# Row maxima in an adaLN block's projection phase: whole chains, more pairs, and the next task for a new K tile

## The chip, the core and the metric

The kernel runs on one core of one Trainium2 chip. The metric is the device time of one execution in microseconds (us). A core has the engines TensorE (PE, with its weight loads PEld), VectorE (DVE), ScalarE (ACT), GpSimd (POOL) and SyncE (SP, which issues most DMAs).

## The reference, cut to what matters

```python
mod = (_silu(c) @ w_mod).reshape(c.shape[0], 6, 1, -1)      # sa, ca, ga, sb, cb, gb
h = _layernorm(x) * (1 + ca) + sa
q, k, v = (h @ wqkv) in 16 heads of 28                       # x: 2048 tokens x 448
p = softmax(q k^T * 28 ** -0.5)                              # over all 2048 keys
x = x + ga * ((p v) @ wo)
h = _layernorm(x) * (1 + cb) + sb
x = x + gb * (gelu(_layernorm(h) @ w1 + b1) @ w2 + b2)       # 448 -> 1792 -> 448
```

All is in fp32. The kernel splits each fp32 operand into a rounded part, hi (fp32r), and the rest, lo, and adds up hi x hi, hi x lo and lo x hi.

## The kernel before, in words

**Phases.** Phase one makes Q, K and V; the attention follows, and the MLP at its end. The 2048 tokens are four blocks of 512 (b = 0 to 3), the 16 heads four groups of four (g = 0 to 3). A group's four heads lie at partitions 0, 32, 64 and 96 (j = 0 to 3).

**Tasks of phase one** (loop at L901). A task of block b makes one tile of Q (kind 0) or K (kind 1) of one group (`qk_task`), or 128 tokens of V (kind 2, `v_task`), by a chain of 11 matmuls on PE (L464, `mm_acc`). Block 0 has 13 tasks, blocks 1 and 2 have 11 each, block 3 has 8; the number within the block is n. The last two tasks of a block but the last make Q and K of group 0 for the next block. In blocks 1 and 2 tasks 5 to 8 are those on V, and tasks 4 to 7 also prepare a piece of the next block's normalised input (`h_chunk`: ACT scales and casts it, POOL makes its lo part). In block 0 the first three chains are computed ahead of the loop. For blocks 2 and 3 the input comes transposed; DVE takes the statistics (`ln1_cols`, L214 and L215) two blocks ahead, one step per task, the last step (`rows_out`) sends mean and scale through DRAM into rows, and POOL applies them (L333, L334) at tasks 1, 2, 4 and 5 (`APPLY_AT`) of the block before.

**Row maxima.** The softmax needs each row's maximum over the keys. It is taken ahead of the attention, from the hi parts: a single maximum (`max_one`) is one matmul of 28 rows (L544, 128 queries against 512 keys of one head) and one DVE reduction (L549). A unit is one group with one block of queries, written (g, qt), in all 16; with 4 blocks of keys, 4 rows of queries and 4 heads there are 1024 maxima. A pair of maxima (`pair_diff`) takes two key blocks A and B at once: a matmul against B - A (`k_diff`, made by POOL), a Relu on ACT (L557), a matmul against A, and one DVE instruction that adds both and reduces (L561): max(A, B) = A + relu(B - A). So a pair costs two matmuls, as two singles do, one ACT and one DVE instruction. `paired` names the units whose first two key blocks go so in phase one; they wait in `pxq`, the others in `mxq`.

**How many, and where.** Behind each chain `emit_task(n, sixth, n_pairs)` puts n maxima's worth of work (P1RATE = 4 in block 0, 5 later; one more, in the PSUM tile `o`, where `sixth` is set and there is a pair): the matmuls of the pairs' differences, then singles, then the pairs' second matmuls. Five PSUM tiles serve them in turn (`mx_ring`: ma, ma, m2, m2, m1). `p1_n` carries its settings. In tasks 1, 3 and 5 of block 1 `emit_mid` puts four more maxima into the middle of the chain. `queue_max` offers a new K tile's maxima; the loop calls it after the next task's `emit_task`, so the offer serves the task after that.

**Attention.** 256 steps, 16 for each unit, at each a tile of scores (L1453, 12 matmuls), two exponentials (L1466), and the product with V of the step before (L1408). What maxima phase one left are done inside the steps. Up to step RING - 1 a step has four single matmuls, or three and a pair's difference. From step RING = 121 (the ring form) it has one single and one double, two matmuls into a two-bank tile with one DVE reduction of 1024 columns (L757). In the last steps there are none left and three score tiles take turns. `load_hi` brings the hi tiles of the next group from DRAM and lets their maxima be used 3 steps later, or 5 in the ring form.

Of the kernel before, what the change touches and what calls it, by code (L numbers as in the profile page):

```python
# [14 lines left out]
F32R = mybir.dt.float32r  # L15
# [19 lines left out]
APPLY_AT = (1, 2, 4, 5)  # L35
RING = 121
MOD_AT = 124
# [10 lines left out]
def tile_adaln_block(ctx: ExitStack, tc: tile.TileContext, x, x_t, wqkv, wo, w1, b1, w2, b2, c, w_mod, out):  # L48
# [410 lines left out]

    def mm_acc(p, terms, mid=None):  # L460
        for i, (a, b) in enumerate(terms):
            if mid and i == len(terms) // 2:
                mid()
            pe.matmul(p, a, b, start=(i == 0), stop=(i == len(terms) - 1))  # L464
# [18 lines left out]
    def qk_task(b, kind, g, begun=None):  # L483
        p, ts = begun or qk_terms(b, kind, g)
        if begun is None:
            mm_acc(p, ts, p1_n[3])
        emit_task(*p1_n[:3])
        if g == 0:
            tg = ("kh" if kind else "qh") + str(b)
            hi = sb.tile([128, 512], F32R, tag=tg, name=nm(tg), bufs=1)  # L490
            (kh_sb if kind else qh_sb)[(g, b)] = hi
        elif g == 1 and b < 2:

            hi = sbt("raw" if kind else "osb", [128, 512], F32R, bufs=3 if kind else 2)
            (kh_sb if kind else qh_sb)[(g, b)] = hi
        else:
            hi = sbt("hi", [128, 512], F32R, bufs=3)
        full = sbt("full", [128, 512], bufs=3)
        lo = sbt("lo", [128, 512], F32R, bufs=3)
        act.copy(full, p)  # L500

        def split():
            (act.copy if b else dve.tensor_copy)(hi, full)
            if kind == 1 and (g, b) == (0, 1):
                k_diff.append(sbt("raw", [128, 512], F32R, bufs=3))
                pool.tensor_tensor(out=k_diff[0], in0=f(hi), in1=f(kh_sb[(0, 0)]), op=ALU.subtract)
            pool.tensor_tensor(out=lo, in0=full, in1=f(hi), op=ALU.subtract)
            sl = slice(b * 512, (b + 1) * 512)
            for part, t in enumerate((hi, lo)):
                sp.dma_start(f(dscr[kind][part][g])[:, sl], f(t))  # L510

            if b < 3 or g == 0 or (kind, g) == (0, 1):
                put_spare()
            spare.append((kind, g, sl))

        return split

    def v_task(b, t, p):
# [3 lines left out]
            lambda k: hh(k)[:, ts], lambda k: hl(k)[:, ts], lambda k: wv[0][:, k, :], lambda k: wv[1][:, k, :],  # L522
        ), p1_n[3] if phase1[0] else None)
        if phase1[0]:
# [7 lines left out]
    pxq = []  # L532
    k_diff = []
    paired = ((0, 1), (0, 2), (0, 3))
    px_no = [0]
# [17 lines left out]
    def pair_diff(g, qt, i, j):  # L553
        m = max_mm(g, qt, i, j, k_diff[0])
        r = d0(1 + px_no[0] % 3)
# [208 lines left out]
    def emit_task(n, sixth, n_pairs):  # L764
# [8 lines left out]
        for x in range(n_ops - len(pairs)):  # L773
            if mxq:
                near = [m for m in mxq[:24] if not p1_n[4] or m[:2] == mxq[0][:2]]
                want = free[x % len(free)] if free else x % 4
# [21 lines left out]
    p1_n = [0, False, 1, None, False]  # L798

# [94 lines left out]
    for b in range(NB):  # L894
# [11 lines left out]
        for n, (tb, kind, g) in enumerate(tasks):  # L906
# [8 lines left out]

            k = n - (6, 4, 4, 4)[b]
# [694 lines left out]
```

## Time and profile before

| | |
|---|---|
| time, median of 3 runs | 1087.91 us (1087.47 to 1088.52) |
| the profiled execution's time | 1088.08 us |
| its span | 1086.3 us |
| busy: PE, DVE, ACT, POOL | 1077.9, 801.0, 691.2, 251.2 us |
| phase one ends (first score matmul) | 158.67 us |
| granted TensorE clock | 1.0 |

A row of a timeline gives the start, the length, the engine, the line, what is written and read, the shapes and the number merged; in brackets stands the idle time ahead of it and what ended it. Matmuls overlap, so PE's lengths do not add up; starts are what counts. A row of windows gives the stretch, its length, then busy time and count of PE, PEld, DVE, ACT and POOL, then clock, DMA share and GB/s.

### The profile page before, as it was taken

How to read it: one execution, taken by the hardware profiler on the slowest of the kernel's cores; microseconds unless marked ns; L12 is line 12 of the kernel's file. 1: busy time of each engine (PE TensorE's matmuls, PEld its weight loads, DVE VectorE, ACT ScalarE, POOL GpSimd, SP SyncE). 2: the span in 40 equal slices, each digit the busy share in tenths (PEclk: the TensorE clock that was granted, in tenths of full speed). 3: DMA queues.
4: the chain of work that ended last, by engine and by line, in shares of the span. 5: the costliest groups of instructions: out<-in, count | busy, mean ns of one | idle time of the engine just before them, and what ended most of it. 6: DMA issues, size and time to landing. Idle time of an engine off the chain costs nothing.

```text
span 1086.3 us, 20646 instructions
## 1 busy us (share of the span) xinstructions
PE 1077.9 (99%) x8199; PEld 656.5 (60%) x8199; DVE 801.0 (74%) x1374; ACT 691.2 (64%) x870; POOL 251.2 (23%) x228
## 2 busy tenths in 40 slices
PE   9999999999999999999999999999999999999998
PEld 6766674444444444444444444544488888888887
DVE  6979788989989899988888988585655565464422
ACT  4645758888888888888888888687943321211111
POOL 1583730011011011033221410217114032061000
PEclk9999999999999999999999999999999999999999
DMA  9454271112122211243322423111433301002000
GB/s 311 175 180 134 104 226 47 52 56 58 56 81 65 73 30 46 60 130 100 94 57 89 119 64 92 58 32 59 123 121 96 104 35 48 27 34 73 34 1 34
DMA packets 60759, 91.73 MB, mean 84 GB/s; under 512 B 14159, under 2 KB 26086, under 8 KB 60650
## 3 DMA queue, kind: packets, MB, share of 16 engines
q1 hardware_dynamic: 60178, 89.67, 26.8%
q8 instruction: 64, 1.05, 0.4%
q10 hardware_dynamic: 148, 0.46, 0.1%
q14 instruction: 33, 0.27, 0.1%
q0 software_dynamic: 336, 0.28, 0.1%
HBM read 62.54 MB, written 29.51 MB: 85 GB/s over the span
## 4 chain that ended last, share of the span: by engine, by line
PE 87%; ACT 0%; issue 0%; DVE 0%; ACTq 0%
PE s L1453 24%; PE o L1408 23%; PE m L464 17%; PE m L544 6%; PE s L1545 3%; PE s L1547 3%; PE s L1546 3%; PE pa L464 2%; PE s L544 2%; PE t L1547 1%; PE t L1545 1%; PE t L1546 1%; PE ma L544 0%; PE m L340 0%; DVE mxp L549 0%
## 5 line engine op out<-in xcount | busy, mean ns | idle before, releaser
L549 DVE TENSOR_REDUCE mxp<-m 128x1 f32<-128x512 f32 x583 | 376.3, 686 | 74.9 <-PE m L544 57.5
L1453 PE MATMUL s<-slot_b,slot_a 28*128 28x512 f32 (+1 forms) x3072 | 358.2, 425 | 0.1
L1453 PEld LDWEIGHTS s<-slot_b,slot_a 28*128 28x128 f32 (+1 forms) x3072 | 211.3, 183 | 175.3 <-ACT slot_c L1466 97.4
L544 PE MATMUL m<-kh,qh 28*128 28x512 f32 x607 | 221.1, 471 | 0.4 <-ACT full L840 0.3
L1466 ACT ACTIVATE slot_c<-s 128x1024 f32<-128x1024 f32 x170 | 174.7, 1028 | 52.0 <-PE s L1453 51.2
L1408 PE MATMUL o<-slot_c,v 128*32 128x512 f32 x680 | 178.9, 605 | 0.0
L1501 ACT ACTIVATE full<-m,b_col 128x512 f32<-128x512 f32 x56 | 38.5, 688 | 192.8 <-PE m L464 184.4
L757 DVE TENSOR_REDUCE mxp<-s 128x2 f32<-128x1024 f32 x107 | 131.1, 1226 | 5.7 <-PE s L544 0.7
L1408 PE MATMUL o<-slot_c1h,v 128*32 128x512 f32 x512 | 134.7, 605 | 0.0
L1408 PE MATMUL o<-slot_c0h,v 128*32 128x512 f32 x508 | 133.6, 605 | 0.0
L1466 ACT ACTIVATE slot_c1h<-s 128x1024 f32<-128x1024 f32 x128 | 130.8, 1022 | 0.0
L1466 ACT ACTIVATE slot_c0h<-s 128x1024 f32<-128x1024 f32 x127 | 130.7, 1029 | 0.0
L1466 ACT ACTIVATE slot_d<-s 128x1024 f32<-128x1024 f32 x86 | 88.3, 1027 | 27.3 <-PE s L1453 26.7
L1128 POOL TENSOR_TENSOR osb<-osb,osb 128x512 f32<-128x512 f32 x16 | 20.5, 1281 | 342.6 <-DMA osb<-drec 245.1
L544 PEld LDWEIGHTS m<-kh,qh 28*128 28x128 f32 x607 | 88.4, 181 | 15.5 <-DVE mxp L549 12.7
L1504 DVE CAST hi<-full 128x512 fp32r<-128x512 f32 x42 | 19.0, 453 | 102.1 <-ACT full L1501 102.0
L1408 PE MATMUL o<-slot_d,v 128*32 128x512 f32 x344 | 90.5, 605 | 0.4 <-ACT osb L1372 0.4
L1505 DVE TENSOR_TENSOR lo<-full,hi 128x512 fp32r<-128x512 f32 x56 | 46.2, 826 | 28.6 <-ACT hi L1504 24.5
L464 PE MATMUL m<-y,slot_a 128*128 128x512 f32 x160 | 59.7, 389 | 0.0
L721 DVE CUSTOM_DVE_ANT_0 slot_d0i<-m,slot_d0i 128x512 f32<-128x512 f32 x55 | 38.0, 692 | 15.8 <-PE m L544 11.8
L1408 PEld LDWEIGHTS o<-slot_c,v 128*32 128x32 f32 x680 | 24.5, 108 | 39.8 <-issue 37.5
L544 PE MATMUL s<-kh,qh 28*128 28x512 f32 x214 | 47.2, 436 | 0.0
(365 smaller groups left out, 1825.9 us busy)
## 6 DMA issues: line engine op xcount, KB each, us to landing
slot_b<-d SPq DMA_DIRECT2D x32, 256.0 KB
slot_a<-d SPq DMA_DIRECT2D x32, 256.0 KB
d<-lo SPq DMA_DIRECT2D x28, 256.0 KB
d<-hi SPq DMA_DIRECT2D x16, 256.0 KB
osb<-drec SPq DMA_DIRECT2D x15, 256.0 KB
out_dram<-xn SPq DMA_DIRECT2D x16, 224.0 KB
raw<-in_B_w_dram SPq DMA_DIRECT2D x14, 224.0 KB
qh<-d SPq DMA_DIRECT2D x12, 256.0 KB
```

Of the source, the lines that this page charges most:

```text
L464: pe.matmul(p, a, b, start=(i == 0), stop=(i == len(terms) - 1))
L544: pe.matmul(m, qh_sb[(g, qt)][js, i * 128 : (i + 1) * 128], k[js, :], start=True, stop=True)
L549: dve.tensor_reduce(out=mxp[(g, qt)][:, i, j, cch : cch + 1], in_=m, op=ALU.max, axis=AX.X)
L757: dve.tensor_reduce(out=mxp[(g, qt)][:, i, j : j + 2, cch], in_=t, op=ALU.max, axis=AX.X)
L1408: pe.matmul(o[32 * j : 32 * j + 32, :], v_sb[kt // 4][:, kt % 4, 4 * g + j, :], p[j // 2][:, j % 2, :], start=(kt == 0), stop=(kt == NKT - 1),
L1453: pe.matmul(s2[:, jj, :], ks[rows_, kp, kc], qs[rows_, qp, :], start=(term == 0), stop=(term == 2))
L1466: act.activation(pt[hf], s2, AF.Exp, scale=SCALE)
L1501: act.activation(gf, p, AF.Gelu_apprx_tanh, bias=b1_col[:, i : i + 1])
L1505: dve.tensor_tensor(out=glo, in0=gf, in1=f(ghi), op=ALU.subtract)
L1545: pe.matmul(pp, ghi[:, ts], w_hi, start=(m == 0), stop=False)
L1546: pe.matmul(pp, ghi[:, ts], w_lo, start=False, stop=False)
L1547: pe.matmul(pp, glo[:, ts], w_hi, start=False, stop=(m == NFT - 1))
```

## The change

- No maxima inside chains: `emit_mid` goes.
- Pairs also for unit 5, which is (1, 1), with a second difference `k_diff[1]` in a buffer of its own; row 3 of unit (0, 1) is done by singles instead.
- The number of pairs per task is a table (`P1PAIRS`): block 1 has 0, 3, 3, 3, 1, 2, 2, 2, 3, 2, 2 where it had one each, block 2 two each as before, block 3 as before but for its last task, which does nothing. The sixth maximum is allowed in all of block 1.
- A K tile's maxima are offered ahead of the task that follows it; the new Q tile of block 1 offers (0, 1, 0) at once.
- The statistics of block 3 are taken at tasks 1, 2, 3, 8 and 9 of block 1 instead of 6 to 10. Those of block 2 stay.
- RING is 112 instead of 121.

In all, phase one has 55 pairs (42 before) and does 209 of the 1024 maxima (201 before); the attention has 52 pairs (55) and 116 doubles (107).

```diff
-RING = 121
+STAT_AT = ({7: 0, 8: 1, 9: 2, 10: 3, 11: 4}, {1: 0, 2: 1, 3: 2, 8: 3, 9: 4})
+P1PAIRS = ((0,) * 13, (0, 3, 3, 3, 1, 2, 2, 2, 3, 2, 2), (2,) * 11, (1,) * 5 + (3,) * 3)
+RING = 112
...
         if begun is None:
-            mm_acc(p, ts, p1_n[3])
+            mm_acc(p, ts)
         emit_task(*p1_n[:3])
...
-            if kind == 1 and (g, b) == (0, 1):
-                k_diff.append(sbt("raw", [128, 512], F32R, bufs=3))
-                pool.tensor_tensor(out=k_diff[0], in0=f(hi), in1=f(kh_sb[(0, 0)]), op=ALU.subtract)
+            if kind == 1 and b == 1 and g < 2:
+                k_diff[g] = sbt("k_diff", [128, 512], F32R) if g else sbt("raw", [128, 512], F32R, bufs=3)
+                pool.tensor_tensor(out=k_diff[g], in0=f(hi), in1=f(kh_sb[(g, 0)]), op=ALU.subtract)
...
-    paired = ((0, 1), (0, 2), (0, 3))
+    paired = ((0, 1), (0, 2), (0, 3), (1, 1))
+    alone = {(0, 1): (3,)}
...
-            return m[:2] != (0, 0), -m[0], m[1:]
+            return m[:2] != (0, 0), m[:2] != (0, 1) or m[2] > 1, -m[0], m[1:]
...
+        own = range(4)
         if (g, qt) in paired and cch < 2:
+            own = alone.get((g, qt), ())
             if cch == 1:
-                pxq.extend((g, qt, i, j) for i in range(4) for j in range(4))
-            return
-        for i in range(4):
+                pxq.extend((g, qt, i, j) for i in range(4) if i not in own for j in range(4))
+        for i in own:
...
-    def emit_mid():
-        for j in range(4):
-            fits = [x for x, m in enumerate(mxq[:24]) if m[4] == j]
-            if fits:
-                m = mxq.pop(fits[0])
-                max_one(*m)
-                count(*m[:2], [m[2]])
...
-            p1_n[1] = b != 1 or n > 7
-            p1_n[2] = (3 if n > 4 else 1) if b == 3 else 2 if b == 2 and p1_n[1] else 1
-            p1_n[3] = emit_mid if (b, n) in ((1, 1), (1, 3), (1, 5)) else None
-            p1_n[4] = not more
-            p1_n[0] -= p1_n[3] is not None
+            p1_n[1:] = b > 0, P1PAIRS[b][n], not more
+            for item in ready:
+                queue_max(*item)
             if kind < 2:
...
+                if (tb, kind, g) == (1, 0, 0):
+                    newq = [(0, 1, 0)]
...
-            for item in ready:
-                queue_max(*item)
...
-                n_stat = n - (7, 6, 99)[b]
-                if 0 <= n_stat < 5:
-                    cols_of[b + 2][0][n_stat]()
+                if b < 2 and n in STAT_AT[b]:
+                    cols_of[b + 2][0][STAT_AT[b][n]]()
```

**PE, block 0, task 3.** `pa` is the chain's PSUM tile, `ma` and `m` those of the maxima, `slot_b` the normalised input, `slot_a` the weights, `kh` and `qh` the hi tiles of K and Q of group 0. Before:

```order
L464 MATMUL pa_391<-slot_b_63_272,slot_a3h_143 128x512
L464 MATMUL pa_391<-slot_b_63_272,slot_a2h_141 128x512
L464 MATMUL pa_421<-slot_b_63_272,slot_a_32_138 128x512
L464 MATMUL pa_421<-slot_b_63_272,slot_a_33_139 128x512
L464 MATMUL pa_421<-slot_b_63_272,slot_a_32_138 128x512
```

and now:

```order
L464 MATMUL pa_391<-slot_b_63_272,slot_a3h_143 128x512
L464 MATMUL pa_391<-slot_b_63_272,slot_a2h_141 128x512
L545 MATMUL ma_404<-kh_87_379,qh_73_341 128x512
L545 MATMUL ma_407<-kh_87_379,qh_73_341 128x512
L545 MATMUL m_94_410<-kh_87_379,qh_73_341 128x512
L545 MATMUL m_95_413<-kh_87_379,qh_73_341 128x512
L464 MATMUL pa_434<-slot_b_63_272,slot_a_32_138 128x512
```

The four maxima of the first K tile stand between the chains of tasks 3 and 4, where the second followed the first at once.

**DVE, the same place.** `kh` is the K tile's cast; `slot_e` are V's weights, `raw` the K tile of group 1, `mxp` the maxima. Before:

```order
L503 CAST osb_356<-full_357 128x512
L503 CAST kh_87_379<-full_380 128x512
L209 TENSOR_TENSOR slot_e_39_145<-slot_v_27_115,slot_e_38_144 128x448 x2
L503 CAST raw_403<-full_404 128x512
L549 TENSOR_REDUCE mxp_433<-ma_434 128x1
```

and now:

```order
L503 CAST osb_356<-full_357 128x512
L503 CAST kh_87_379<-full_380 128x512
L211 TENSOR_TENSOR slot_e_39_145<-slot_v_27_115,slot_e_38_144 128x448
L550 TENSOR_REDUCE mxp_403<-ma_404 128x1
L550 TENSOR_REDUCE mxp_403<-ma_407 128x1
L550 TENSOR_REDUCE mxp_403<-m_94_410 128x1
```

The cast of the K tile has kept its place; the reductions follow two instructions behind it.

**PE, block 1, task 1.** `kh_177` and `raw` are K of block 1 and the difference of two K tiles. Before, the second half of the chain comes after four maxima:

```order
L464 MATMUL pa_793<-slot_c0h_529,slot_a2h_141 128x512
L544 MATMUL m_186_799<-kh_177_759,qh_73_341 128x512
L544 MATMUL m_187_802<-kh_177_759,qh_73_341 128x512
L544 MATMUL m_188_805<-kh_177_759,qh_73_341 128x512
L544 MATMUL ma_808<-kh_177_759,qh_73_341 128x512
L464 MATMUL pa_793<-slot_c0h_529,slot_a3h_143 128x512
```

and now the chain is whole and three pairs stand behind it:

```order
L464 MATMUL pa_822<-slot_c0h_541,slot_a2h_141 128x512
L545 MATMUL ma_834<-raw_778,qh_171_728 128x512
L545 MATMUL m_197_837<-raw_778,qh_171_728 128x512
L545 MATMUL m_198_840<-raw_778,qh_171_728 128x512
L545 MATMUL m_199_843<-kh_87_379,qh_171_728 128x512
L545 MATMUL ma_846<-kh_87_379,qh_171_728 128x512
L545 MATMUL o_849<-kh_87_379,qh_171_728 128x512
```

Three differences and three second matmuls took the place of the four singles inside and the four behind.

More of the change, by code (lines that the diff above doesn't have):

```diff
@@ L458, in put_last_rows, with mm_acc @@
         sp.dma_start(ones_d.rearrange("j (q n) -> j q n", n=256), ones[:, None, :].broadcast_to([4, 8, 256]))
-    def mm_acc(p, terms, mid=None):
+    def mm_acc(p, terms):
         for i, (a, b) in enumerate(terms):
-            if mid and i == len(terms) // 2:
-                mid()
             pe.matmul(p, a, b, start=(i == 0), stop=(i == len(terms) - 1))
@@ L522, in v_task @@
             lambda k: hh(k)[:, ts], lambda k: hl(k)[:, ts], lambda k: wv[0][:, k, :], lambda k: wv[1][:, k, :],
-        ), p1_n[3] if phase1[0] else None)
+        ))
         if phase1[0]:
@@ L532, in tile_adaln_block @@
     pxq = []
-    k_diff = []
-    paired = ((0, 1), (0, 2), (0, 3))
+    k_diff = {}
+    paired = ((0, 1), (0, 2), (0, 3), (1, 1))
+    alone = {(0, 1): (3,)}
     px_no = [0]
@@ L553, in pair_diff @@
     def pair_diff(g, qt, i, j):
-        m = max_mm(g, qt, i, j, k_diff[0])
+        m = max_mm(g, qt, i, j, k_diff[g])
         r = d0(1 + px_no[0] % 3)
@@ L774, in emit_task @@
             if mxq:
-                near = [m for m in mxq[:24] if not p1_n[4] or m[:2] == mxq[0][:2]]
+                near = [m for m in mxq[:24] if not p1_n[3] or m[:2] == mxq[0][:2]]
                 want = free[x % len(free)] if free else x % 4
@@ L787, in emit_task @@
             count(g, qt, [0, 1])
-    def emit_mid():
-        for j in range(4):
-            fits = [x for x, m in enumerate(mxq[:24]) if m[4] == j]
-            if fits:
-                m = mxq.pop(fits[0])
-                max_one(*m)
-                count(*m[:2], [m[2]])
-    p1_n = [0, False, 1, None, False]
+    p1_n = [0, False, 1, False]
     def finish_max(g, qt):
@@ L914, in tile_adaln_block @@
                 p1_n[0] = 0
-            k = n - (6, 4, 4, 4)[b]
-            p1_n[1] = b != 1 or n > 7
-            p1_n[2] = (3 if n > 4 else 1) if b == 3 else 2 if b == 2 and p1_n[1] else 1
-            p1_n[3] = emit_mid if (b, n) in ((1, 1), (1, 3), (1, 5)) else None
-            p1_n[4] = not more
-            p1_n[0] -= p1_n[3] is not None
+            p1_n[1:] = b > 0, P1PAIRS[b][n], not more
+            for item in ready:
+                queue_max(*item)
             if kind < 2:
```

## The prediction

> **What bounds the kernel now.** I read the windows by stage first, then the timeline of TensorE (PE) through phase one, then those of ACT, VectorE (DVE) and GpSimd (POOL) where PE waits. The windows (length, busy time and count of PE, PEld, DVE, ACT, POOL, clock, DMA), then the same view for the exponentials of L1466 alone, two of which make a step of the attention:
>
> ```profile
> 200.00:440.00 240.00, 239.94 (x2298) 113.18 (x2292) 217.43 (x403) 205.88 (x242) 21.58 (x20) 1.00 0.20 58
> 463.00:620.00 157.00, 156.68 (x1593) 67.26 (x1593) 135.04 (x158) 135.60 (x143) 50.10 (x39) 1.00 0.33 97
> ...
> 200.00:440.00 240.00, 185.86 (x192) 1.00 0.20 58
> 481.00:663.00 182.00, 155.37 (x160) 1.00 0.33 95
> ```
>
> PE reads as full in both stretches, yet a step is 240 / 96 = 2.50 us before the ring form (step 121) and 182 / 80 = 2.275 us in it. So PE's busy share doesn't say what it can still give; the distances between its instructions do. Phase one, block 1, chains and what lies between them (start, length, x count):
>
> ```profile
> 55.52 1.07 PE L464 MATMUL pa<-slot_c,slot_a 128*128 128x512 f32 x4
> ...
> 58.01 1.07 PE L464 MATMUL pa<-slot_c,slot_a 128*128 128x512 f32 x4
> ...
> 62.13 1.18 PE L464 MATMUL pa<-slot_c,slot_a 128*128 128x512 f32 x4
> ...
> 65.49 1.20 PE L464 MATMUL pa<-slot_c,slot_a 128*128 128x512 f32 x4
> ...
> 70.17 1.19 PE L464 MATMUL pa<-slot_c,slot_a 128*128 128x512 f32 x4
> ...
> 73.55 1.08 PE L464 MATMUL pa<-slot_e,slot_c 128*128 128x448 f32 x4
> ...
> 78.23 1.08 PE L464 MATMUL pa<-slot_e,slot_c 128*128 128x448 f32 x4
> ...
> 87.48 2.12 PE L464 MATMUL pa<-slot_b,slot_a 128*128 128x512 f32 x8
> ...
> 91.35 1.19 PE L464 MATMUL pa<-slot_b,slot_a 128*128 128x512 f32 x4
> ...
> 95.09 2.11 PE L464 MATMUL pa<-slot_b,slot_a 128*128 128x512 f32 x8
> ...
> 99.11 1.21 PE L464 MATMUL pa<-slot_b,slot_a 128*128 128x512 f32 x4
> ...
> 102.54 2.12 PE L464 MATMUL pa<-slot_b,slot_a 128*128 128x512 f32 x8
> ...
> 105.93 1.20 PE L464 MATMUL pa<-slot_b,slot_a 128*128 128x512 f32 x4
> ```
>
> From one chain's start to the next's: a chain alone 2.49 (55.52 to 58.01); with five maxima 3.36 (62.13 to 65.49); with six, where nothing waits, 3.39 (102.54 to 105.93). Tasks 1, 3 and 5 of block 1, which carry maxima inside the chain, take 4.12, 4.68 and 4.68; tasks 9 and 10 take 3.87 and 3.74, and task 0 of block 2 takes 4.02. These six are where phase one loses time.
>
> **The tasks of block 1.** The last stall of phase one, and the length of a task on V:
>
> ```profile
> 121.96 1.90 PE L464 MATMUL pa<-slot_e,slot_b 128*128 128x448 f32 x8
> ...
> 125.06 1.21 PE L464 MATMUL pa<-slot_c,slot_a 128*128 128x512 f32 x4
> ...
> 127.89 0.73 PE L464 MATMUL pa<-slot_c0h,slot_a 128*128 128x512 f32 x2 [0.46 <-POOL slot_c0h L349]
> 128.55 0.50 PE L544 MATMUL ma<-raw,qh 28*128 28x512 f32 x1
> ...
> 129.22 1.19 PE L464 MATMUL pa<-slot_c,slot_a 128*128 128x512 f32 x4
> ...
> 131.94 0.49 PE L544 MATMUL ma<-raw,qh 28*128 28x512 f32 x1
> ```
>
> A task on V with six maxima is 3.10 (121.96 to 125.06). With the chains whole and six maxima behind each, tasks 1, 3, 9, 10 and task 0 of block 2 come to 3.39, task 5 to 3.10: 0.73 + 1.29 + 1.58 + 0.48 + 0.35 + 0.63 = **5.06 gained**, if DVE and ACT keep up. The prices for that:
>
> ```profile
> 61.57 0.68 DVE L549 TENSOR_REDUCE mxp<-ma 128x1 f32<-128x512 f32 x1
> ...
> 63.38 0.68 DVE L561 CUSTOM_DVE_ANT_0 slot_d<-m,slot_d 128x512 f32<-128x512 f32 x1
> ...
> 81.19 0.60 ACT L557 ACTIVATE slot_d0i<-ma 128x512 f32<-128x512 f32 x1 [1.03 <-PE m L544]
> ...
> 82.95 0.62 ACT L345 CAST slot_b<-full 128x512 fp32r<-128x512 f32 x1
> ...
> 149.01 0.49 PE L544 MATMUL ma<-raw,qh 28*128 28x512 f32 x1
> ...
> 149.90 1.09 PE L464 MATMUL pa<-slot_e,slot_c 128*128 128x448 f32 x4
> ```
>
> On DVE a pair, two maxima, costs 0.68 plus its accumulator read of about 0.1, a single 0.68, so at most: three pairs 2.3, two pairs and two singles 2.9, one pair and four singles 3.5; back to back they come closer (a single starts every 0.6). Before, one pair, four singles and a statistic of 0.8 stood in tasks 8 to 10, over 3.39, and hence their waits; now no such task carries a statistic. ACT has 2.4 in a V task with one pair (81.19 to 83.57), so 2.9 with two, under 3.10. What no row of block 1 shows is three pairs in a task. The nearest are block 3's, where such a group takes 0.89 (149.01 to 149.90) against 0.66 undisturbed (3.39 less a chain of 2.72, 129.22 to 131.94). Bounds for four tasks: 0 to 0.9, below nothing excluded because 0.66 is PE's own work. I take **0.3 lost**: block 3's waits come behind 3.10-us V tasks; three of the four here have 3.39.
>
> The other tasks go from five maxima to six: 3.36 against 3.39, nothing. Block 3's statistics move off tasks 6 to 10: its rows leave one task, some 3.4 us, sooner. POOL waits for them (first row of the second pair):
>
> ```profile
> 64.43 1.27 POOL L333 TENSOR_TENSOR xn<-xn,slot_v 128x512 f32<-128x512 f32 x1 [3.56 <-DMA slot_v<-ln_dr]
> ...
> 86.79 1.29 POOL L349 TENSOR_TENSOR slot_b<-full,slot_b 64x512 fp32r<-64x512 f32 x1 [1.85 <-ACT slot_b L345]
> ...
> 106.89 1.30 POOL L333 TENSOR_TENSOR xn<-xn,slot_v 128x512 f32<-128x512 f32 x1 [4.97 <-DMA slot_v<-ln_dr]
> ...
> 126.55 1.28 POOL L349 TENSOR_TENSOR slot_c0h<-full,slot_c0h 64x512 fp32r<-64x512 f32 x1
> ```
>
> POOL starts 106.89, ends this work at 127.83, and PE's chain of block 2, task 9 waits for it: 3.49 (125.06 to 128.55) against 2.72. A lead of 3.4 covers that: **0.77 gained**. Next late there is ACT, which hands POOL its pieces.
>
> **What is added.** The first K tile's maxima move from behind task 4 to behind task 3 of block 0:
>
> ```profile
> 24.77 1.07 PE L464 MATMUL pa<-slot_b,slot_a 128*128 128x512 f32 x4
> ...
> 27.26 1.98 PE L464 MATMUL pa<-slot_b,slot_a 128*128 128x512 f32 x8
> ...
> 30.28 1.19 PE L464 MATMUL pa<-slot_b,slot_a 128*128 128x512 f32 x4
> ...
> 33.42 2.11 PE L464 MATMUL pa<-slot_b,slot_a 128*128 128x512 f32 x8
> ...
> 28.07 0.42 DVE L503 CAST kh<-full 128x512 fp32r<-128x512 f32 x1
> ```
>
> Task 3's chain (24.77) ends at 27.35, but the K tile is cast by DVE until 28.49, behind the statistics of block 1, which the change leaves there. PE stands with task 4's chain queued behind: **1.15 lost**. The group itself is only moved, for task 11 then finds the queue empty. Task 12 gains a group of four (the offered tile (0,1,0)), 3.14 (30.28 to 33.42) less 2.49 = **0.65 lost**; task 0 of block 1 a group of five, 3.36 less 2.49 = **0.87 lost**. The new difference of K tiles on POOL (about 1.28, as its like) delays block 2's pieces, and the offer delays their rows by about 1.3; the last piece would be ready near 87.9, and PE would want it near 88.6. Margin 0.7: nothing, but thin.
>
> A rule weighs against these two groups. The rows price a group by what waits: 0.65 to 0.89 plain, up to 1.5 in the split chains. The Trainium skill, TensorEngine Tiling (Array Packing), Key Properties, says that each change of tiling mode drains the array, whatever the number of matmuls. By it alone three groups leave and two come, the six tasks gain one group of 0.65 and no more, and the sum would be 0.65 + 0.77 - 1.15 + 2.3 = 2.6, or 1085.3; the split tasks' 4.68 with eight maxima against 3.36 with five, waits for buffers that DVE frees, are not in the rule.
>
> **The ring form from step 112.** Steps 112 to 120 now run as before step 121 (ACT, exponentials that open 112 and 121):
>
> ```profile
> 442.49 1.02 ACT L1466 ACTIVATE slot_c<-s 128x1024 f32<-128x1024 f32 x1
> ...
> 465.29 1.02 ACT L1466 ACTIVATE slot_c<-s 128x1024 f32<-128x1024 f32 x1 [0.80 <-PE s L1453]
> ```
>
> They take 22.80; nine ring steps take 9 x 2.275 = 20.48: **2.3 gained** (2.0 by the mean of 2.50). All later steps carry the same matmuls as before. The maxima for it come from phase one, which does eight more, and from its thirteen more pairs, which cost PE nothing.
>
> **Sum.** Phase one 5.06 + 0.77 - 0.3 - 1.15 - 0.65 - 0.87 = 2.86; with the ring 2.3, 5.2 us. The profiled execution took 1088.08 (span 1086.3), the median is 0.17 lower: 1088.08 - 5.2 - 0.17 = **1082.7**. About 0.2% (2.2 us) can be told from no change.
>
> **Rivals.**
> - The K tile's wait is hidden, because DVE is sooner there: 1081.5. Against it, DVE has no gap ahead of that cast. Chance 0.08.
> - Block 1 gives part back: POOL's last piece comes late (margin 0.7), or three pairs press on DVE and ACT at every task. 0.3 for each of ten tasks, or POOL late by 2, gives 1084.5 to 1085.7. For it: ACT at 2.9 of 3.10. Chance 0.20.
> - PE is the bound, at 239.94 of 240, with as many matmuls as before: no change, 1087.9. Against it stand 2.50 and 2.275 at equal busy shares. The Trainium skill, Perfetto Trace Analysis, Identifying the Most-Contended Engine, calls matmul busy time a poor measure; the two windows agree. Chance 0.07.
> - Slower: in the ring K tiles are used from five steps after their load is asked for, 11.4 us at 2.275. If a load took x, each of the last group's four tiles would hold PE for x - 11.4. From x = 12.7 that eats the 5.2; at 14 it is 1093. Against it: POOL's wait of 4.97 at 106.89 covers a write and a read back. Chance 0.05.
>
> **How the numbers follow.** The forecast has 0.60. Its own range is 1081.8 (no cost of three pairs and a shorter wait) to 1083.5 (three pairs at 0.9, the ring at 2.0). The range takes in the hidden wait and most of the second rival: 1080.9 to 1085.5. Faster by over 0.2% (below 1085.7): 0.60 + 0.08 + 0.20 = 0.88; within, 0.07; slower 0.05.
>
> **What would show it.** Right: PE idle about 1.1 us ahead of the first maxima near 28.5; every task of block 1 at 3.4 or 3.1; no wait for POOL in block 2's task 9; phase one ends near 155.8, not 158.67; the double reductions start nine steps sooner. Wrong: gaps ahead of maxima in tasks 1 to 8 of block 1, a chain of task 9 waiting for POOL, steps 112 to 120 still at 2.5, or PE waiting for a tile's load in the ring.

## The result, and the profile after

The changed kernel takes 1082.31 us (1081.51 to 1082.45, 4 runs) against 1087.81 of the kernel before on the same chip: a ratio of 0.9947 (95% interval 0.993 to 0.9964). A repeat gave 1081.30 (1080.49 to 1082.34, 5 runs), 0.9939 (0.9926 to 0.9951). So the same kernel moves by 1.0 us from one measurement to the next; what is smaller than that is read from the traces below and not from the times. The profiled execution took 1082.24, its span is 1080.5.

Four distances split a span: the lead up to the first chain of the loop over tasks, phase one from there to the first score matmul, the attention from the first step's exponential to the last step's, and the rest behind it (a microsecond or so between score and exponential is left out).

| profile | lead | phase one | attention | rest | span |
|---|---|---|---|---|---|
| before | 24.77 | 133.91 | 625.85 | 300.71 | 1086.3 |
| after | 24.24 | 132.63 | 621.97 | 300.36 | 1080.5 |
| after, repeat | 24.01 | 131.69 | 622.07 | 300.33 | 1079.2 |

Of 5.8 us (after) the attention gave 3.9, phase one 1.3 and the lead 0.5; in the repeat phase one gave 2.2. The lead holds nothing of the change: over the fourteen profiles of this study it lies between 23.60 and 25.14.

Timeline of TensorE in the changed kernel, the first matmuls of the chains of block 1's tasks 0 to 6, 9 and 10 and of block 2's tasks 0 and 1:

```profile
56.73 1.19 PE L464 MATMUL pa<-slot_c,slot_a 128*128 128x512 f32 x4
...
60.11 1.19 PE L464 MATMUL pa<-slot_c,slot_a 128*128 128x512 f32 x4
...
63.55 1.20 PE L464 MATMUL pa<-slot_c,slot_a 128*128 128x512 f32 x4
...
66.94 1.20 PE L464 MATMUL pa<-slot_c,slot_a 128*128 128x512 f32 x4
...
73.73 1.08 PE L464 MATMUL pa<-slot_e,slot_c 128*128 128x448 f32 x4
...
77.22 1.08 PE L464 MATMUL pa<-slot_e,slot_c 128*128 128x448 f32 x4
...
86.57 2.11 PE L464 MATMUL pa<-slot_b,slot_a 128*128 128x512 f32 x8
...
89.95 1.19 PE L464 MATMUL pa<-slot_b,slot_a 128*128 128x512 f32 x4
...
93.33 2.11 PE L464 MATMUL pa<-slot_b,slot_a 128*128 128x512 f32 x8
...
96.71 1.19 PE L464 MATMUL pa<-slot_b,slot_a 128*128 128x512 f32 x4
```

Task 0 takes 3.38, task 1 3.44, task 2 3.39, tasks 9, 10 and block 2's task 0 3.38 each; from task 1's chain to block 2's task 1 it is 36.60, where before it was 41.10 (58.01 to 99.11). Only task 5, on V, is off: 3.49 (73.73 to 77.22) instead of 3.10.

Block 0, task 3, TensorE and then VectorE:

```profile
24.24 1.07 PE L464 MATMUL pa<-slot_b,slot_a 128*128 128x512 f32 x4
...
28.06 0.49 PE L545 MATMUL ma<-kh,qh 28*128 28x512 f32 x2 [1.16 <-DVE kh L503]
...
28.49 2.12 PE L464 MATMUL pa<-slot_b,slot_a 128*128 128x512 f32 x8
```
```profile
27.49 0.42 DVE L503 CAST kh<-full 128x512 fp32r<-128x512 f32 x1
```

TensorE stands 1.16 for the K tile's cast: the forecast wait. Block 2, task 9, in the first profile and in the repeat:

```profile
122.61 1.21 PE L464 MATMUL pa<-slot_c,slot_a 128*128 128x512 f32 x4
...
125.45 0.73 PE L464 MATMUL pa<-slot_c0h,slot_a 128*128 128x512 f32 x2 [0.48 <-POOL slot_c0h L351]
...
126.78 1.20 PE L464 MATMUL pa<-slot_c,slot_a 128*128 128x512 f32 x4
```
```profile
122.30 1.19 PE L464 MATMUL pa<-slot_c,slot_a 128*128 128x512 f32 x4
...
125.92 1.20 PE L464 MATMUL pa<-slot_c,slot_a 128*128 128x512 f32 x4
```

4.17 from chain to chain (4.16 before), 3.62 in the repeat, 3.38 undisturbed: the stall that was to go, 0.79, is there, and 0.24 of it in the repeat. Why, SyncE's queue and GpSimd show (transfers by their issue; `r` holds the rows ready to be sent, `slot_v` the rows as GpSimd needs them):

```profile
92.06 0.34 SPq L510 DMA_DIRECT2D d<-qh  x1
93.43 2.68 SPq L510 DMA_DIRECT2D d<-lo  x1
...
97.71 1.42 SPq L329 DMA_DIRECT2D ln_dr<-r  x4
```
```profile
104.43 1.30 POOL L335 TENSOR_TENSOR xn<-xn,slot_v 128x512 f32<-128x512 f32 x1 [4.27 <-DMA slot_v<-ln_dr]
```
```profile
92.35 0.21 DVE L326 STREAM_TRANSPOSE r<-st 128x32 f32<-128x32 f32 x1
```

VectorE has the rows ready at 92.56, 6.2 sooner than before (98.75), but they leave at 97.71, behind a Q tile's parts: SyncE waits 6.6 for ScalarE's cast of that tile before 92.06, then for its low part until 93.43, and that part takes 2.68 to go out. From GpSimd's start to task 9's chain it is 18.18 (104.43 to 122.61); before it was 18.17 (106.89 to 125.06). So GpSimd starts 2.46 sooner, and TensorE comes to task 9 2.45 sooner: no lead is left.

The steps' exponentials on ScalarE: the first step, steps 112 and 121, the last step:

```profile
158.13 1.03 ACT L1456 ACTIVATE slot_d<-s 128x1024 f32<-128x1024 f32 x1 [0.92 <-DVE mxp L550]
...
440.40 1.03 ACT L1456 ACTIVATE slot_c<-s 128x1024 f32<-128x1024 f32 x1 [0.71 <-PE s L1443]
...
460.65 1.03 ACT L1456 ACTIVATE slot_c<-s 128x1024 f32<-128x1024 f32 x1 [0.33 <-PE s L1443]
...
780.10 1.02 ACT L1456 ACTIVATE slot_d<-s 128x1024 f32<-128x1024 f32 x1
```

Steps 112 to 120 take 20.25 (22.80 before), so 2.55 of the attention's 3.9 lie there; the rest is spread over other steps.

### The profile page after: what moved, and what is told of

Same layout as the page of the kernel before. It is cut to its first block, busy times and chain, and to the rows that moved or that the text cites. A ratio compares the mean times of both kernels' runs of the same rounds, so it can differ in the third digit from the quotient of the medians.

```text
span 1080.5 us, 20678 instructions
## 1 busy us (share of the span) xinstructions
PE 1069.8 (99%) x8199; PEld 650.7 (60%) x8199; DVE 796.8 (74%) x1365; ACT 697.3 (65%) x880; POOL 252.4 (23%) x229
## 4 chain that ended last, share of the span: by engine, by line
PE 87%; ACT 1%; DMA 0%; DVE 0%; issue 0%; SPq 0%; DVEq 0%; ACTq 0%
PE s L1443 23%; PE o L1398 23%; PE m L464 17%; PE m L545 6%; PE s L1535 3%; PE s L1537 3%; PE s L1536 3%; PE s L545 2%; PE pa L464 2%; PE t L1537 1%; PE t L1535 1%; PE t L1536 1%; PE ma L545 0%; DMA slot_a<-d 0%; DVE mxp L550 0%
## 5 line engine op out<-in xcount | busy, mean ns | idle before, releaser
L550 DVE TENSOR_REDUCE mxp<-m 128x1 f32<-128x512 f32 x554 | 359.0, 687 | 72.5 <-PE m L545 60.8
L545 PE MATMUL m<-kh,qh 28*128 28x512 f32 x594 | 217.3, 473 | 0.5 <-ACT full L834 0.3
L759 DVE TENSOR_REDUCE mxp<-s 128x2 f32<-128x1024 f32 x116 | 142.2, 1226 | 5.0
L545 PEld LDWEIGHTS m<-kh,qh 28*128 28x128 f32 x594 | 86.1, 181 | 13.9 <-DVE mxp L550 11.5
L545 PE MATMUL s<-kh,qh 28*128 28x512 f32 x232 | 51.8, 442 | 0.0
```

The costliest lines, as they stand in the source:

```text
L545: pe.matmul(m, qh_sb[(g, qt)][js, i * 128 : (i + 1) * 128], k[js, :], start=True, stop=True)
L550: dve.tensor_reduce(out=mxp[(g, qt)][:, i, j, cch : cch + 1], in_=m, op=ALU.max, axis=AX.X)
L759: dve.tensor_reduce(out=mxp[(g, qt)][:, i, j : j + 2, cch], in_=t, op=ALU.max, axis=AX.X)
```

## The experiments

Each is timed against the kernel before, on the same chip. The four distances of each profile:

| run | median us | ratio (95%) | lead | phase one | attention | rest |
|---|---|---|---|---|---|---|
| e1_ring121 | 1083.76 | 0.9963 (0.9951, 0.9976) | 24.39 | 133.01 | 623.49 | 300.30 |
| e2_before_ring112 | 1090.64 | 1.0029 (1.0018, 1.0039) | 24.25 | 134.05 | 628.81 | 300.64 |
| e3_rows_early | 1083.74 | 0.996 (0.9946, 0.9974) | 24.12 | 135.97 | 622.20 | 300.34 |
| e4_kh_act | 1081.87 | 0.9943 (0.9931, 0.9956) | 25.14 | 131.66 | 622.30 | 300.32 |
| e5_rows_first | 1080.90 | 0.9935 (0.9921, 0.9949) | 24.55 | 131.46 | 622.08 | 300.36 |
| e6_split | 1087.08 | 0.9993 (0.9984, 1.0002) | 24.26 | 135.52 | 623.53 | 300.22 |
| e7_old_offer | 1084.51 | 0.9973 (0.9963, 0.9983) | 24.30 | 129.90 | 626.70 | 300.77 |
| e8_together | 1088.73 | 1.0009 (1.0, 1.0018) | 23.60 | 137.04 | 623.66 | 300.30 |
| e9_best | 1081.08 | 0.9937 (0.9923, 0.995) | 24.04 | 130.62 | 622.82 | 300.70 |
| e10_old_stats | 1086.50 | 0.9986 (0.9977, 0.9995) | 24.28 | 137.07 | 621.98 | 300.37 |
| e11_after_again | 1081.30 | 0.9939 (0.9926, 0.9951) | 24.01 | 131.69 | 622.07 | 300.33 |
| e12_small_pieces | 1080.98 | 0.9938 (0.9924, 0.9951) | 24.75 | 132.00 | 623.63 | 300.24 |

### The ring form without and with its maxima

```diff
-RING = 112
+RING = 121
```

> The changed kernel with the ring form put back to step 121; everything in phase one stays as changed. Theory (the forecast's): steps 112 to 120 go back from 20.25 us to 22.8, so 2.5 are lost; its nine spared ring steps leave fewer maxima over, and the kernel runs out of them four steps sooner (step 233 instead of 237, in the stretch where the output is projected), which may give some tenths back: 1084.2 to 1084.9, with steps 112 to 120 at 22.8. Rival (TensorE is full in either form, and all 5.5 us come from phase one): 1082.3 within 0.4, with the nine steps' loss made up elsewhere.

Measured 1083.76, 1.4 to 2.5 above the changed kernel. The exponentials of steps 112 and 121:

```profile
440.55 1.02 ACT L1456 ACTIVATE slot_c<-s 128x1024 f32<-128x1024 f32 x1
...
463.36 1.02 ACT L1456 ACTIVATE slot_c<-s 128x1024 f32<-128x1024 f32 x1 [1.03 <-PE s L1443]
```

22.81, so the nine steps cost what they cost before. But the attention is only 1.52 longer (623.49 against 621.97), as unit 14, whose maxima now run out sooner, takes 0.8 less. And it is still 2.36 shorter than before, with the ring form where it was. Fewer maxima explain little of that: only unit 14 has clearly fewer in the trace (9 singles for 18), and it is 0.26 shorter (44.05 for 44.31); the other 2.1 lie in units with the same counts. The theory's loss was right at its place, its total a little high; the rival falls.

The other way round, the kernel before with the ring form moved alone:

```diff
-RING = 121
+RING = 112
```

> The kernel before with one number changed, the ring form from step 112 instead of 121. Theory (the ring form is paid for with maxima done in phase one): a ring step does three maxima where a step of the first form does four, so nine are left over; the order of the program shows a fourth maximum in eight ring steps of units 7 to 14. A step with four costs about 0.25 more (2.50 against 2.25), 8 x 0.25 = 2.0, so of 2.5 gained only 0.5 stays: 1086.9 to 1087.6. Rival (the ring form alone is the gain, a fourth maximum rides in it for nothing): 1085.3 within 0.4.

Measured 1090.64: slower than the kernel before, and slower than either expectation allowed. Exponentials of four ring steps of unit 8, and the matmul of the fourth maximum in the first of them:

```profile
503.76 1.02 ACT L1466 ACTIVATE slot_c<-s 128x1024 f32<-128x1024 f32 x1 [0.24 <-PE s L1453]
...
506.50 1.02 ACT L1466 ACTIVATE slot_c<-s 128x1024 f32<-128x1024 f32 x1 [0.80 <-PE m L544]
...
508.88 1.02 ACT L1466 ACTIVATE slot_d<-s 128x1024 f32<-128x1024 f32 x1 [0.44 <-PE s L1453]
...
511.37 1.02 ACT L1466 ACTIVATE slot_c<-s 128x1024 f32<-128x1024 f32 x1 [0.55 <-PE s L1453]
```
```profile
504.06 0.49 PE L544 MATMUL m<-kh,qh 28*128 28x512 f32 x1
```

Three steps of 2.74, 2.38 and 2.49 follow one another, 7.61 for 6.75 of plain ring steps (3 x 2.25): a fourth maximum costs 0.86 here, spread over three steps, not the 0.25 that I had put on it. Eight of them eat the 2.5 and 3 more (attention 628.81 against 625.85), 0.7 each. So the ring form pays only with the maxima that phase one takes off the attention: the theory's direction, three times its price.

### The offer of K tiles

The offer behind the task, as before:

```diff
-            for item in ready:
-                queue_max(*item)
             if kind < 2:
...
                 v_task(tb, g, ps_s())
+            for item in ready:
+                queue_max(*item)
```

> The changed kernel with the new K tiles offered where the kernel before does it, behind the task instead of ahead of it. Phase one then does 203 maxima instead of 209, and the order of the program shows a fourth maximum in one ring step of each of units 8 to 13. Theory (the offer pays through the ring): phase one gains the wait of 1.2 and the group of four of 0.65, but a fourth maximum in a ring step costs about 0.7, worked out from the run of the kernel before with the ring from step 112 (628.81 from the first step's exponential to the last's, against 625.85 less 2.5 gained, over eight such steps): 6 x 0.7 = 4.2, together 2.3 slower, 1084.2 to 1085.0. Rival (the offer costs its wait and buys nothing): 1080.4 to 1081.2.

Measured 1084.51. Phase one is 2.73 shorter (129.90 against 132.63), without the wait of 1.16 and with six maxima fewer; the attention is 4.73 longer, 0.8 for each of those six, within the prices that the run above gave; 4.44 of it lie in units 8 to 13, which have one more each and take 0.59 to 0.87 longer. The offer costs what was forecast and earns more in the attention; the rival falls.

### Cut chains

```diff
+            mid_n[0] = emit_half if b == 1 and n in (5, 6, 7, 9, 10) else None
+            if mid_n[0]:
+                p1_n[:3] = 2, True, 1
...
+    def emit_half():
+        emit_task(2, True, 1)
...
         for i, (a, b) in enumerate(terms):
+            if mid and i == len(terms) // 2:
+                mid()
```

> The changed kernel with the group of six maxima of block 1's tasks 5, 6, 7, 9 and 10 cut in two, three in the middle of the chain and three behind it; the maxima and their pairs stay the same. Theory A (the split chains of the kernel before cost their 4.1 to 4.7 us because eight maxima waited for buffers that VectorE frees): with six the cut costs nothing, tasks stay at 3.4 and 3.1, 1082.3. Theory B (each change between the two kinds of matmul on TensorE has its own price, whatever the number of matmuls): a group of four takes 0.65 from chain to chain and a group of six 0.66, so two groups of three take 1.2 to 1.3 instead of 0.66, 5 x 0.6 = 3.0: 1085.0 to 1085.6, with tasks at 4.0 and 3.7 and no wait in them.

Measured 1087.08. TensorE in block 1's task 5 and the start of task 6:

```profile
73.71 1.08 PE L466 MATMUL pa<-slot_e,slot_c 128*128 128x448 f32 x4
...
74.92 0.49 PE L547 MATMUL ma<-raw,qh 28*128 28x512 f32 x1
...
75.58 0.47 PE L466 MATMUL pa<-slot_e,slot_c0h 128*128 128x448 f32 x1
...
76.99 0.49 PE L547 MATMUL m<-raw,qh 28*128 28x512 f32 x1
...
77.80 1.08 PE L466 MATMUL pa<-slot_e,slot_c 128*128 128x448 f32 x4
```

The first half of the group takes 0.66 (74.92 to 75.58), as long as the whole of six does in one piece, and no row waits in front of it; the second 0.81, with 0.20 for a buffer. The task takes 4.09 instead of 3.49. In tasks 6 and 7 it is 3.97 and 3.94 instead of 3.10, in 9 and 10 4.25 instead of 3.38. Theory B was right, and low: 0.85 for each cut. What of it the change between the two kinds of matmul costs is not shown: each half holds a pair, whose two matmuls use the same head's rows and stand one behind the other (79.02 and 79.36 in task 6), while a group of four on four heads takes 0.44 in one piece (31.23 to 31.67 in block 0 of the changed kernel). (Of the 4.2 by which the span exceeds that of the changed kernel, 2.9 lie in phase one, which escapes the stall of block 2's task 9 here, and 1.6 in the attention, which has the same counts of maxima, 1.3 of them in unit 4; that part I can't account for.) The Trainium skill, TensorEngine Tiling (Array Packing), Key Properties, says that changing the tiling mode drains TensorE; it gives no price, and here a cut, which adds two such changes and divides a group, shows 0.85.

### The stall at block 2's task 9

Statistics sooner still:

```diff
-{1: 0, 2: 1, 3: 2, 8: 3, 9: 4}
+{1: 0, 2: 1, 3: 2, 7: 3, 8: 4}
```

> The changed kernel with block 1's last two steps of statistics one task sooner again (tasks 7 and 8 for 8 and 9), which puts the six transfers of the rows on SyncE's queue ahead of the next block's Q and K tiles. Theory (the stall of block 2's task 9 stayed, 3.51 us against 2.72, because the rows stood on that queue behind tile transfers that wait for GpSimd and ScalarE, from 92.6 when they were ready to 97.7): GpSimd starts on block 3 some 4 us sooner, task 9 comes to 2.7, 0.8 gained: 1081.5 (1081.2 to 1081.8). Rival (GpSimd is then held by ScalarE's pieces or by its own queue, 21 us of work without a gap): the stall stays, 1082.3, or it is 0.3 worse, because VectorE has a statistic of 0.8 in a task that has 3.1 in all.

Measured 1083.74, worse (the profiled execution, 1085.47, is the slowest of the five). Task 9 of block 2 does come to 2.70 plus its group, but the rows, first on SyncE's queue, wait there for their own statistic, with the transfers of many small pieces (`ones_d`) and then a tile's parts behind them, and each of these is long in going out:

```profile
93.51 3.17 SPq L460 DMA_DIRECT2D ones_d<-slot_d  x1
96.72 4.28 SPq L510 DMA_DIRECT2D d<-qh  x1
```
```profile
114.34 0.49 PE L545 MATMUL ma<-raw,qh 28*128 28x512 f32 x1 [0.81 <-ACT slot_d0h L558]
```

The tiles' buffers come free late, ScalarE's cast waits 4.08 for one, the difference of a pair is queued behind it, and TensorE waits for that. Block 1's task 9 also lost 0.9, for GpSimd's last piece, behind the statistic's arithmetic. Neither theory had this: the stall went as the first said, and more came in two other places.

Only the queue's order, no statistic:

```diff
-            for part, t in enumerate((hi, lo)):
-                sp.dma_start(f(dscr[kind][part][g])[:, sl], f(t))
+            def out():
+                for part, t in enumerate((hi, lo)):
+                    sp.dma_start(f(dscr[kind][part][g])[:, sl], f(t))
+            if (kind, g, b) == (0, 0, 2):
+                held.append(out)
+            else:
+                out()
...
                     cols_of[b + 2][0][STAT_AT[b][n]]()
+                while held:
+                    held.pop()()
```

> The changed kernel with one thing moved on SyncE's queue: in block 1's task 9 the two transfers of the next block's Q tile come behind the six of the rows, instead of ahead of them; no statistic is moved. Theory (the rows wait on the queue behind a tile whose low part GpSimd delivers at 93.4): they leave near 92.6 instead of 97.7, GpSimd starts on block 3 near 100.2 instead of 104.4, task 9 of block 2 comes to 2.7 instead of 3.51, and 0.8 is gained: 1081.3 to 1081.7. First rival (the queue itself is held in these microseconds by the transfers of many small pieces that went out at 84.6, so that whoever is first waits): the rows leave as late as before, 1082.3. Second rival (as in the run with the statistics in tasks 7 and 8, what is pushed back is worth more): a wait for the buffers of the tiles' parts, over 1082.8.

Measured 1080.90, the lowest median, and the stall is gone (122.91 to 126.28, 3.37). But GpSimd hardly has the rows sooner:

```profile
85.60 8.51 SPq L448 DMA_DIRECT2D d<-d  x2
94.21 3.37 SPq L329 DMA_DIRECT2D ln_dr<-r  x4
```

The transfer behind the small pieces takes 8.51 to go out: the first rival's mechanism. The rows leave at 94.21 instead of 97.71, but their four transfers take 3.37 instead of 1.42. GpSimd starts at 103.43, as in the plain repeat (103.55). The stall of 0.24 that the repeat still has is gone mainly because TensorE comes to task 9 0.61 later here (122.91 against 122.30), after a lead that is 0.54 longer. And the time can't be told from the repeat's 1081.30. So the edit is not shown to gain anything.

The statistics back where they were:

```diff
-{1: 0, 2: 1, 3: 2, 8: 3, 9: 4}
+{6: 0, 7: 1, 8: 2, 9: 3, 10: 4}
```

> The changed kernel with the statistics of block 3 back in block 1's tasks 6 to 10, as in the kernel before, and the queue as changed. Theory (the queue, not the statistics, sets when the rows leave): the last statistic comes one task later, the rows leave about as before the change, and GpSimd's last piece with them; task 9 of block 2 stays near 3.5, at most a microsecond longer, while VectorE has a statistic more in tasks 6 and 7, 0.8 in 3.1: 1082.0 to 1083.4. Rival (the sooner statistics of the change had kept the stall from growing by the whole 3.4): task 9 near 6, 1085 to 1086.

Measured 1086.50: my theory fell, the rival is right in size, though not in place: task 9 takes 3.37, and the loss lies in tasks 6 and 7, 6.50 and 5.30 instead of 3.11 and 3.10. The rows leave 3.1 later, GpSimd starts at 107.54 instead of 104.43, ScalarE waits for it with the pairs' differences queued behind, and TensorE for those (ScalarE, TensorE, then windows with granted clock):

```profile
115.36 0.81 ACT L363 ACTIVATE full<-xn,cols 128x512 f32<-128x512 f32 x1 [3.28 <-POOL lo L507]
```
```profile
117.74 0.66 PE L545 MATMUL ma<-raw,qh 28*128 28x512 f32 x1 [1.94 <-ACT slot_d L558]
```
```profile
117.00:119.00 2.00, 1.26 (x5) 0.72 (x5) 1.27 (x4) 2.00 (x5) 1.92 (x2) 0.73 0.55 196
119.00:121.00 2.00, 2.00 (x7) 1.39 (x5) 1.83 (x5) 1.97 (x5) 2.00 (x5) 0.50 0.60 219
```

Phase one is 4.4 longer than in the changed kernel. Of the 5.6 that tasks 6 and 7 lose, 1.94 is the wait; most of the rest falls in the stretch at half the clock behind it. In the kernel before the same statistics cost a stall of 0.77, and the likely reason, which no run shows by itself, is that its slow tasks left the queue the time: from the rows' leaving to task 9's chain it is 24.7 before (100.34 to 125.06) and 24.9 after (97.71 to 122.61).

### The other waits, and all together

The K tile's cast on ScalarE:

```diff
-            (act.copy if b else dve.tensor_copy)(hi, full)
+            (act.copy if b or (kind, g) == (1, 0) else dve.tensor_copy)(hi, full)
```

> The changed kernel with the first K tile's cast (block 0, task 2) on ScalarE, right behind its copy, instead of VectorE, where it stands behind four statistics of block 1. Theory (TensorE waits 1.16 us ahead of 28.06 for nothing but that cast): the maxima start at 26.9, 1.1 to 1.2 gained, 1081.1 to 1081.3. Rival (something behind it is late too: VectorE's reductions cannot start before 27.8 and hold the buffers, or ScalarE's casts of the V weights come 0.6 later): part or all of it is lost again by task 6 of block 0, 1081.8 to 1082.5.

Measured 1081.87. The chain of task 3 with its group takes 3.02 instead of 4.25 (25.14 to 28.16), 1.2 gained, and two groups later 0.7 is lost:

```profile
34.08 0.50 PE L545 MATMUL m<-kh,qh 28*128 28x512 f32 x2
...
35.20 1.20 PE L464 MATMUL pa<-slot_b,slot_a 128*128 128x512 f32 x4
```

That group takes 1.12 (34.08 to 35.20) instead of 0.43: VectorE, held by four statistics until 27.8 and then by the weights of V, frees the buffers late. The rival was right about more than half, and the time can't be told from the changed kernel's 1082.31 and 1081.30.

That edit, the rows' order of e5, and two pairs instead of one in some tasks:

```diff
-P1PAIRS = ((0,) * 13, (0, 3, 3, 3, 1, 2, 2, 2, 3, 2, 2), (2,) * 11, (1,) * 5 + (3,) * 3)
+P1PAIRS = ((0,) * 13, (0, 3, 3, 3, 2, 2, 2, 2, 3, 2, 2), (2,) * 11, (1,) + (2,) * 4 + (3,) * 3)
```

> The changed kernel with the K tile's cast on ScalarE, the Q tile's transfers behind the rows, and one pair more in block 1's task 4 and in tasks 1 to 4 of block 3 (whose neighbours' groups wait for VectorE, 0.4 at block 1's task 5 and 0.1 to 0.4 at four tasks of block 3). Phase one does three maxima more. Theory (these waits add up on TensorE): 0.4 as the cast gave by itself, 0.8 for the rows, 0.4 and 0.6 for the pairs, 0.2 from maxima that end a step sooner: 1079.9 to 1080.6. Rival (what one wait gives the next one takes, since the blocks' rows come by transfers of their own clock): 1081.3 to 1082.0.

Measured 1088.73, a miss on all sides:

```profile
160.64 0.79 PE L1452 MATMUL s<-slot_b,slot_a 29*128 29x512 f32 x2 [6.38 <-DMA slot_b<-full]
```
```profile
157.15 2.31 SPq L606 DMA_DIRECT2D slot_b<-full  x4
```

More pairs in block 3 mean fewer singles, and unit (0, 0) is done by singles alone: its maxima, which the first scores need as a row of their Q tile, leave at 157.15 instead of 147.51, and the attention starts 6.4 late. Block 3's one pair per task is what gets the first unit done in time. Without that edit:

```diff
-P1PAIRS = ((0,) * 13, (0, 3, 3, 3, 2, 2, 2, 2, 3, 2, 2), (2,) * 11, (1,) + (2,) * 4 + (3,) * 3)
+P1PAIRS = ((0,) * 13, (0, 3, 3, 3, 2, 2, 2, 2, 3, 2, 2), (2,) * 11, (1,) * 5 + (3,) * 3)
```

> The changed kernel with three of the edits of the runs before: the Q tile's transfers behind the rows, the K tile's cast on ScalarE, and two pairs instead of one in block 1's task 4; block 3 keeps its pairs as changed, so that the first unit's maxima are done in time. Theory (the three waits lie in different places and add up): 1080.9 as measured with the rows first, less 0.4 for the cast as it measured alone, less 0.4 for the wait at block 1's task 5: 1079.8 to 1080.4, with tasks 3 of block 0 at 3.0, 5 of block 1 at 3.1 and 9 of block 2 at 3.38. Rival (the rows' edit is all that lasts, the others come back as waits behind them): 1080.7 to 1081.3.

Measured 1081.08. No task waits any more where these edits aimed (the group two behind the cast loses its 0.7 as before), block 1's task 5 takes 3.10, and phase one is 1.1 shorter than in the repeat of the changed kernel; but it ends with 208 maxima instead of 209 and the attention is 0.75 longer. Beside it the changed kernel itself:

> The changed kernel as it is, beside the two others on the same chip, for the size of what a repeat moves: by every theory 1082.3 within 0.4, and a profile with the same waits at the same tasks.

Measured 1081.30, with the same waits but for task 9 of block 2 (3.62). And the small pieces three tasks sooner, with the pairs as changed:

```diff
-            if b == 1 and n == 8:
+            if b == 1 and n == 5:
                 put_last_rows()
```

> The changed kernel with the K tile's cast on ScalarE, the Q tile's transfers behind the rows, and the three transfers of many small pieces (84.6 in the changed kernel) sent three tasks sooner, in block 1's task 5 instead of 8; the pairs as changed, so that phase one keeps its 209 maxima. Theory (it was those three that held SyncE's queue: the transfer behind them took 8.51 to go out when the rows stood first): with nothing held the rows leave at 92.6, 5 sooner than in the changed kernel, GpSimd starts on block 3 at 99 to 101 instead of 103.4 to 104.4, task 9 of block 2 takes 3.38; phase one some 131.0, the attention 622.0, in all 1080.0 to 1080.8. Rival (the queue is held by something else, or what is held now are the loads of x behind them, which block 3 needs): the rows leave at 94 or later and GpSimd starts at 103 or later, 1080.8 to 1082, or a wait in block 2, over 1082.5.

Measured 1080.98 (the profiled execution, 1083.68, is the slowest of the five). The queue is still behind with tiles, the last of the pieces goes out only 1.2 sooner (83.44 for 84.62), and now the loads of x behind them are held:

```profile
83.44 3.56 SPq L460 DMA_DIRECT2D ones_d<-slot_d  x1
87.04 7.50 SPq L297 DMA_DIRECT2D xn<-in_x_cols_dram  x3
...
95.90 1.43 SPq L329 DMA_DIRECT2D ln_dr<-r  x4
```

The rows leave at 95.90 and GpSimd starts at 103.57: the rival. No version here is shown to beat the changed kernel; 1080.90, 1080.98, 1081.08 and its own 1081.30 have intervals that lie over one another.

## Why the prediction was right, and where it was not

The time was forecast at 1082.7 and measured at 1082.31 and 1081.30. The sum came out by terms that missed in both directions, and that it came so near is in part luck: phase one gave 1.6 less than forecast, the attention 1.6 more, and the lead, which holds nothing of the change, another 0.5.

- **Tasks of block 1**, 5.06 less 0.3 for three pairs: 4.50 measured (41.10 less 36.60). The tasks with three pairs (1, 2, 3 and 8) take 3.44, 3.39, 3.40 and 3.13, together 0.1 over, not 0.3. What is missing is 0.39 at task 5, where the maximum in `o` waits for a reduction that VectorE ends at 76.74, because task 4 has one pair and four singles and finds a statistic of task 3 ahead of them. With two pairs there, in e9, the wait is gone.
- **"The rows price a group by what waits"**: this step failed in part. The forecast put the loss of tasks 1, 3 and 5 on waits for buffers, against the rule on changes of mode. e6 shows 0.85 for a cut chain with next to nothing late, so a cut has a price without any wait. But the waits were there too. In the kernel before, the group of four inside the chain takes 0.44 in task 1 (59.23 to 59.67), 0.92 in task 3 (66.84 to 67.76) and 1.06 in task 5 (74.77 to 75.83). The groups behind these three chains take 0.86, 0.82 and 0.98, where one of five that doesn't wait takes 0.66 (64.83 to 65.49). What TensorE's weight loads wait for in task 3 (in task 5 it is 0.42 for the same, at 75.40):

```profile
67.33 0.18 PEld L544 LDWEIGHTS m<-kh,qh 28*128 28x128 f32 x1 [0.30 <-DVE mxp L549]
...
69.74 0.18 PEld L544 LDWEIGHTS m<-kh,qh 28*128 28x128 f32 x1 [0.20 <-DVE mxp L549]
```

  As an estimate from these rows, 1.8 of the 3.60 that these tasks lost are waits (0.48 + 0.62 + 0.20 + 0.16 + 0.32), and the three cuts themselves make the other 1.8, 0.6 each. Tasks 9, 10 and block 2's task 0 (1.49 gained) had no cuts; there it was waiting.
- **The offer's wait of 1.15, the group of four, the group of five**: 1.16 for the wait; block 0 from task 3 on is 1.74 longer (30.75 before, from 24.77 to 55.52; 32.49 after, from 24.24 to 56.73) where 1.80 was forecast, and block 1's task 0 0.89 where 0.87 was. Right.
- **A lead of 3.4 covers the stall, 0.77 gained**: failed. In the first profile nothing was gained, in the repeat 0.54. The step took the lead of the statistics for that of GpSimd. It left out the queue by which the rows leave, where they stood 5.15 behind other transfers (92.56 to 97.71), and that the tasks became shorter too: GpSimd started 2.46 sooner, task 9 came 2.45 sooner. e10 shows what the sooner statistics are worth: not a stall less, but some 4 us that the shorter tasks would otherwise have run into, more than half of it in the stretch of slow clock behind the wait.
- **Phase one, 2.86**: 1.27, and 2.22 in the repeat. Beside the stall and task 5, block 3 and the first scores lost 0.64 (0.32 in the repeat), at groups that wait for VectorE and, by 0.2, at a K tile's load.
- **The ring form, 2.3**: 2.55 in steps 112 to 120. But the sum has nothing for the other steps, and the attention gained 3.9, of which 2.36 come without the ring form (e1) and 1.52 from it. The eight maxima that phase one takes off show in unit 14 alone, by 0.26; where the rest of the 2.36 comes from is not shown. e2 shows that the ring form without those eight loses 3. The forecast named phase one as where the ring's maxima come from and did not price them.
- **The rivals**: the K tile's wait was not hidden; TensorE was not the bound; no step of the ring waits for a tile's load. Of the second, the late piece of GpSimd came true in block 2 rather than block 1, and e10 shows how near it was.

What stays open: why some single ring steps of the kernel before (2.4 to 2.8 in units 8, 9, 11 and 12) are plain in e1 with the same counts of maxima. They make about half of the 2.1 above (1.1); no run tried them by themselves.

## What to carry to other kernels

When work is moved off a full engine, price it where it was and where it lands: a fourth maximum cost 0.7 to 0.9 in a ring step, so six or eight of them outweighed the better form of nine steps. When tasks get shorter, every producer with its own clock, a DMA queue above all, comes nearer to being late: follow each of its transfers, and what is queued ahead of it, and don't count the lead of the instruction that fills it. And repeat the profile before believing a gain under a microsecond.

## What the runs showed of the hardware that was not expected

**A queue behind small pieces.** Three transfers of many small pieces hold what is issued behind them on SyncE's queue: 8.51 in e5 for two transfers that take 1.29 at 81.20, 7.50 in e12, 4.28 in e3. In the changed kernel the next one waits 6.6 for its own tile, and the one behind it takes 2.68. Behind the pieces the DMA engines move 25 to 26 GB/s (88 to 92 in the changed kernel), after 301 between 84 and 86.

**The clock after a wait.** In e10 TensorE stands 1.94 and then runs at a granted clock of 0.50 for almost 7 us (118.0 to 124.5; the windows above show the first of it). The same in e12 behind a wait of 0.87 at the attention's start, in a chain on V that takes 3.99 instead of 2.43:

```profile
155.50:158.66 3.16, 2.20 (x18) 1.11 (x17) 1.66 (x5) 1.17 (x2) 0.47 (x1) 1.00 1.03 384
158.66:162.65 3.99, 3.99 (x12) 3.19 (x12) 1.18 (x2) 1.30 (x2) 0.00 (x0) 0.57 0.94 324
```

So does e3 behind its 0.81 (0.56 from 115.50 to 119.36) and e8 behind its 6.38 (0.50 from 160.64 to 165.00). In e8 the clock falls inside the wait, more than 4 us after its start: 1.00 from 157 to 158, 0.50 from 159 to 160. The wait of 1.16 in block 0 of the changed kernel leaves none: its clock stays 1.00. The Trainium skill, TensorE: Matmul & The Clock Gate, Part 1, puts the half clock behind an idle window of about 3.4 us that runs freely; that it strikes after one wait and not after another agrees with a window that runs freely, and e8 fits the length too; but 1.94, 0.87 and 0.81 are far below 3.4, and the measurement decides.
